# Counting the late units of a routed expert kernel in one chain of narrow steps, and turning the third unit's rows two products later

## The chip, the cores and the metric

The kernel runs on one core of a Trainium2 chip. The metric is the device time of one execution in microseconds (us). Three executions of the kernel before took 648.83, 647.14 and 644.44 us; their median is 647.14 us. A further execution was profiled. TensorE is called PE here, VectorE DVE, ScalarE ACT, GpSimd POOL and SyncE SP, as the profile does.

## The reference

An attention block feeds a mixture-of-experts block. All is float32.

```python
# attention: q, k, v are (8, 8, 576, 64); heads 0-3 see the last 32 positions,
# heads 4-7 every fourth of the last 128
attn = softmax(where(mask, q @ k.T / 8, -1e9));  x = (attn @ v) as (8, 576, 512)
# experts: 8 of them, w1 (8, 512, 1024), w2 (8, 1024, 512)
logits = x @ w_gate;  local = sigmoid(x @ w_local)
for b in range(8):
    prev_e = -1
    for s in range(576):
        fresh_e = argmax(logits[b, s])
        if s == 0 or local[b, s] < 0.5: e = fresh_e
        else:                           e = prev_e if prev_e >= 0 else fresh_e
        prev_e = e
        out[b, s] = softmax(logits[b, s])[e] * (relu(x[b, s] @ w1[e]) @ w2[e])
```

So each of 4608 tokens has one expert, and which one is known only once the attention of its batch is done, and for a later token only once its predecessors are.

## The kernel before, in words

**Stages.** First comes the attention, over eight batches. Rows of x go to DRAM (`xd`). After every two batches a group of tokens is routed (`route(g)`, four groups): logits, argmax, the carrying of an expert along a batch, and a running count of tokens for each expert. Then the experts' work is done in units. A unit is a set of rows of one expert, gathered from `xd` by an indirect DMA on POOL's queue (`fetch`, L948 to L961: a one-element memset on DVE, L959, that orders the transfer, and the transfer, L960). Its rows are turned so that features lie along partitions (`turn_rows`, L975: for units 0 to 3 eight PE transposes, L992, into a PSUM bank and one ACT copy, L993, for each 128 rows), multiplied by w1 (`hidden`), by w2 (`output`), scaled by the gate and sent to DRAM with an indirect DMA (`send`).

**Units.** A pair is 256 rows of an expert, a full 128, a half 64, a quarter 32. Pairs use a scheme with seven block products in place of eight (`chain`, L1005): each needs sums of blocks of the weights (`sums_of_weights`), of the rows (`sums_of_rows`, tile `xc`, L924 to L927) or of the hidden values (`hc`), made by DVE. Unit 1 is a pair whose hidden product is the plain one (L1072 to L1082; eight steps m0 to m7, each eight records of the trace). Units 0 and 1 ("early", `FIRST = 2`) are pairs chosen after half of the tokens are routed, so that PE has work while the routing of the last group goes on. All others are "late": 14 pairs, 3 fulls, 2 halves and 4 quarters at most.

**Counting.** `count(late)`, a generator, works out which segment of 128 rows of which expert is which unit's. On every partition stands one pair of expert and segment, and the eight counts lie along the free dimension, so nearly all its instructions have 8 elements. The late one first makes four counts for each expert (pairs, fulls, halves, quarters; L659 to L702), then decides for the partition's own segment (L714 to L738) which column of the table it is, and writes rows of zeros with one 1 (`chosen`). In it each kind has its own scan and its own chain of comparisons, on all 8 experts, and the partition's own expert is picked at the end by a product with a 0/1 row (`C_OF`) and a reduction (L734, L735). `table` then makes PE multiply `chosen` by the experts' numbers (`ep`, L748 and L750), `tokens` multiplies it by the lists of rows (`fp`, L801 to L809), and DVE turns that into row numbers (L816 to L833), which the gathers of units 2 and 3 take. `places` (`fq`, L766; L779 to L784) does so for the gathers of unit 4 and on.

**Order.** On PE and DVE the order of instructions is the order in which the program issues them; ACT, POOL and SP are ordered by the planner. The small steps of routing stand in two lists, `waiting` and `behind`, and `gap()` pops one gather (`fetch_some`) and one step of each. `work_gap` is called after each step of `hidden` and `output`; it first pops one or two sums of blocks from the list `soon`. So the late routing is spread over the steps of units 0 and 1: `total(g)` falls after the sixth product of unit 0's hidden, the first part of `count` after m1 of unit 1, the second part after m2, `table` after m5, `tokens` after m6, `places` after the first of the seven output products of unit 1. While these products run, `k` counts them from 0; at `k == 4` `feed()` (L1388) calls `features(FIRST)`: unit 2's rows are turned and their sums made.

```python
        waiting.extend(... + of(carry) + of(total)
                       ...
                       + now(counted_on) + now(sum_up, *[counted_on] * (PASSES if exact else 1)) + pause * 2
                       + now(lambda: table(True)) + now(late_tokens) + pause + now(places))
```

The whole program exists twice; the second copy (`exact`) is run only if a check on sizes and sums fails.

Of the kernel before, what the change touches and what calls it, by code (L numbers as in the profile page):

```python
# [11 lines left out]
F32 = mybir.dt.float32  # L12
# [101 lines left out]
C_AT = C_UP + 1  # L114
C_PAY = C_AT + 4
C_COL = C_PAY + NG * NJ
C_ALL = C_COL + TRIES


def constants():  # L120

    c = np.zeros((P, C_ALL), np.float32)
    c[:, C_ID:C_TRI] = np.eye(P)
    c[:TB, C_TRI:C_IDX] = np.triu(np.ones((TB, TB)), 1)
    c[:, C_IDX:C_REV] = np.arange(E)
# [87 lines left out]
def whole(ctx, tc, exact, bad, qk, v, wgl, w1, w2, con, msk, qmk, out, cst, wg, ones):  # L213
# [431 lines left out]

    tiles = {}

    def count(late):

        w = "late" if late else "early"  # L650

        def number(name, dtype=F32, shape=[P, E]):
            return sm.tile(shape, dtype, name=f"{name}_{w}")
# [4 lines left out]
        ni, nf = number("ni", I32), number("nf")  # L658
        nc.vector.tensor_scalar(ni, cn, float(ROW - 1) if late else 0.0, None, Alu.add)  # L659
        if late:  # L660
            ki, kf = number("ki", I32), number("kf")
            nc.vector.tensor_scalar(ki, cn, float(SQ - 1), None, Alu.add)
            nc.vector.tensor_scalar(ki, ki, 5, None, Alu.logical_shift_right)
            tiles["over"] = over = sm.tile([1, 5], F32, name="over_late")
            most = sm.tile([1, 1], F32, name="most")
            nc.vector.tensor_reduce(most, cn[0:1], axis=AX.X, op=Alu.max)
            nc.vector.tensor_scalar(over[:, 4:], most, float(SEGS * P), None, Alu.is_gt)
        nc.vector.tensor_scalar(ni, ni, 8, None, Alu.logical_shift_right)
        nc.vector.tensor_copy(nf, ni)
        parts = [nf]  # L670
        if late:

            nc.vector.tensor_copy(kf, ki)
            nc.vector.scalar_tensor_tensor(kf, nf, -8.0, kf, Alu.mult, Alu.add)
            full, half, quart = (number(name) for name in ("full", "half", "quart"))
            nc.vector.tensor_scalar(full, kf, 4.0, None, Alu.is_ge)
            nc.vector.scalar_tensor_tensor(kf, full, -4.0, kf, Alu.mult, Alu.add)
            nc.vector.tensor_scalar(half, kf, 2.0, None, Alu.is_ge)
            nc.vector.scalar_tensor_tensor(quart, half, -2.0, kf, Alu.mult, Alu.add)
            nc.vector.tensor_scalar(quart, quart, 0.0, None, Alu.max)  # L680
            left = number("left")
            nc.vector.tensor_tensor(left, nf, tiles["done"], op=Alu.subtract)
            parts = [left, full, half, quart]
        ends, befs = [], []
        for k, part in enumerate(parts):
            ends.append(number(f"end{k}"))
            nc.vector.tensor_tensor_scan(ends[k], part, part, 0.0, Alu.add, Alu.max)
            befs.append(number(f"bef{k}"))
            nc.vector.tensor_tensor(befs[k], ends[k], part, op=Alu.subtract)
        if late:  # L690
            for k, most in enumerate((PAIRS, FULL, HALF, QUART)):
                nc.vector.tensor_scalar(over[:, k:k + 1], ends[k][0:1, E - 1:], float(most), None, Alu.is_gt)
        if not late:
            tiles["done"] = done = number("done")
            nc.vector.tensor_scalar(done, befs[0], -1.0, float(FIRST), Alu.mult, Alu.add)
            nc.vector.tensor_scalar(done, done, 0.0, None, Alu.max)
            nc.vector.tensor_tensor(done, done, nf, op=Alu.min)
            first, ends = None, [(done, befs[0], 0)]
        else:
            first = tiles["done"]  # L700
            nc.vector.tensor_tensor(befs[0], befs[0], first, op=Alu.subtract)
            nc.vector.scalar_tensor_tensor(befs[3], half, float(E), befs[3], Alu.mult, Alu.add)  # L702
            ends = [(nf, befs[0], 0), (full, befs[1], C_FULL), (half, befs[2], C_HALF)]
        cols = TRIES if late else 2 * FIRST
        tiles["chosen", late] = []
        for turn in range(PASSES if exact and late else 1):
            yield
            seg = cst[:, C_S:C_V]
            if turn:
                seg = number("seg", F32, [P, 2])  # L710
                nc.vector.tensor_scalar(seg, cst[:, C_S:C_V], float(turn * SEGS), None, Alu.add)
            seg, seg1 = seg[:, 0:1], seg[:, 1:2]
            to, twice, is_it = number("to"), number("twice"), number("is")
            nc.vector.tensor_scalar(to, befs[0], 2.0, seg1, Alu.mult, Alu.add)  # L714
            if late:
                nc.vector.tensor_scalar(twice, first, 2.0, None, Alu.mult)
                nc.vector.scalar_tensor_tensor(to, twice, seg, to, Alu.is_le, Alu.mult)
            nc.vector.tensor_scalar(twice, ends[0][0], 2.0, None, Alu.mult)
            nc.vector.scalar_tensor_tensor(to, twice, seg, to, Alu.is_gt, Alu.mult)
            for part, bef, c in ends[1:]:  # L720
                nc.vector.scalar_tensor_tensor(is_it, twice, seg, part, Alu.is_equal, Alu.mult)
                nc.vector.scalar_tensor_tensor(is_it, bef, float(c + 1), is_it, Alu.add, Alu.mult)
                nc.vector.tensor_tensor(to, to, is_it, op=Alu.add)
                if c == C_FULL:
                    nc.vector.tensor_tensor(twice, twice, part, op=Alu.add)
            chosen = number(f"chosen{turn}", F32, [P, 2, cols])
            tiles["chosen", late].append(chosen)
            all_of = [(to, 0, C_QUART if late else cols, number("one", F32, [P, 1]))]
            if late:
                nc.vector.scalar_tensor_tensor(is_it, twice, seg, quart, Alu.is_equal, Alu.mult)  # L730
                nc.vector.scalar_tensor_tensor(is_it, befs[3], float(C_QUART + 1), is_it, Alu.add, Alu.mult)
                all_of.append((is_it, C_QUART, TRIES, number("one_quart", F32, [P, 1])))
            for to, a, z, one in all_of:
                nc.vector.tensor_tensor(to, to, cst[:, C_OF:C_S], op=Alu.mult)  # L734
                nc.vector.tensor_reduce(one, to, axis=AX.X, op=Alu.add)  # L735
                for v in range(2):
                    nc.vector.tensor_scalar(chosen[:, v, a:z], cst[:, C_COL + a:C_COL + z], one,
                                            cst[:, C_V + v:C_V + v + 1], Alu.is_equal, Alu.mult)  # L738
        yield

    def table(late):
# [467 lines left out]
    def route(g):  # L1209
# [4 lines left out]
        counts = count(g == NG - 1)  # L1214

        def now(*fs):
            return [lambda: [f() for f in fs]]
# [10 lines left out]
        if g < NG - 1:  # L1228
# [10 lines left out]
            else:  # L1239
# [5 lines left out]
                else:  # L1245
# [255 lines left out]
```

## Time and profile before

| | before |
|---|---|
| median of three executions | 647.14 us (644.44 to 648.83) |
| profiled execution | 646.66 us |
| its span, first to last instruction | 644.9 us |
| mean granted TensorE clock | 0.988 |
| PE busy | 606.5 us (94%) |
| DVE busy | 417.6 us (65%) |
| DMA, mean rate | 217 GB/s |

The times of the trace are counted from the start of the span; 1.76 us of the execution lie outside it. Rows of the timeline give the start, the duration, the engine, the line of the program, the operation, output and inputs with their shapes, and the number of instructions merged into the row; in square brackets stands the idle time of the engine before it and what released it. A float32 matmul of the program shows as two records, a transpose as one.

### The profile page before, as it was taken

What the parts mean: (1) busy time and instruction counts of PE and PEld (TensorE: products, weight loads), DVE (VectorE), ACT (ScalarE), POOL (GpSimd) and SP (SyncE); (2) the same over time, 40 slices, a digit from 0 to 9 for tenths busy, and PEclk for the clock granted to TensorE, in tenths of its full rate; (3) what the DMA queues carried; (4) which work ended last, traced back from release to release, by engine and by line L of the source; (5) the groups of instructions that cost most, each with busy time, mean ns of one, the idle gap of its engine ahead of it and who ended that gap; (6) DMA issues with size and microseconds to landing.
All of it is one profiled execution on the core that took longest, in us unless ns stands there. A gap on an engine that the chain in (4) does not pass through costs nothing.

```text
span 644.9 us, 15442 instructions
## 1 busy us (share of the span) xinstructions
PE 606.5 (94%) x6350; PEld 532.4 (83%) x6350; DVE 417.6 (65%) x976; ACT 176.6 (27%) x320; POOL 243.6 (38%) x219
## 2 busy tenths in 40 slices
PE   6888988889989999999999999999999999999995
PEld 6776776768878899999598998995979999879984
DVE  3768989989596487672747487628292974473851
ACT  2545444353111232212122222121222211213210
POOL 3322142124003655464685435345544455001011
PEclk8999999999999999999999999999999999999998
DMA  9998989398004689677363665855453767470301
GB/s 346 412 326 292 346 279 299 122 363 319 2 33 156 217 321 354 227 257 250 116 238 108 245 240 205 296 188 193 168 187 151 279 229 260 147 270 37 137 33 42
DMA packets 29744, 140.12 MB, mean 217 GB/s; under 512 B 4892, under 2 KB 15260, under 8 KB 23136
## 3 DMA queue, kind: packets, MB, share of 16 engines
q1 hardware_dynamic: 22096, 119.89, 51.0%
q0 software_dynamic: 7568, 19.15, 8.6%
q8 instruction: 52, 0.85, 0.5%
q14 instruction: 28, 0.23, 0.1%
HBM read 145.31 MB, written 19.14 MB: 255 GB/s over the span
## 4 chain that ended last, share of the span: by engine, by line
PE 71%; DVE 15%; issue 6%; DMA 4%; POOL 2%; SPq 0%; ACT 0%; POOLq 0%; DVEq 0%
PE yp L1183 28%; PE hp L1088 20%; PE pv L404 3%; PE hp L1062 3%; PE yp L1171 3%; PE sc L342 3%; DVE pr L348 2%; PE tp L423 2%; DMA vt<-in_v_dram 2%; DVE x L409 1%; POOL xg L960 1%; PE hp L1049 1%; PE yp L1136 1%; PE hp L1039 1%; DMA out_dram<-y,corner 1%
## 5 line engine op out<-in xcount | busy, mean ns | idle before, releaser
L960 POOL DMA_INDIRECT xg<-xd,at x116 | 131.7, 1136 | 142.8 <-DVE xg L959 117.8
L1098 DVE TENSOR_TENSOR h<-hp,h 128x512 f32<-128x512 f32 x45 | 30.7, 688 | 97.2 <-PE hp L1088 97.2
L1183 PE MATMUL yp<-sum,hc 128*128 128x256 f32 x384 | 88.5, 380 | 0.0
L1088 PE MATMUL hp<-xc,sum 128*128 128x128 f32 x720 | 85.6, 275 | 0.0
L1124 POOL DMA_INDIRECT out_dram<-y,tok x35 | 46.9, 1341 | 96.8 <-DVE y L1198 44.7
L1088 PEld LDWEIGHTS hp<-xc,sum 128*128 128x128 f32 x720 | 82.9, 192 | 0.1
L1183 PEld LDWEIGHTS yp<-sum,hc 128*128 128x128 f32 x384 | 72.8, 190 | 9.9
L1198 DVE SCALAR_TENSOR_TENSOR y<-yp,gate,y 128x256 f32<-128x256 f32 x48 | 23.0, 483 | 63.5 <-issue 34.5
L1183 PE MATMUL yp<-raw,h 128*128 128x256 f32 x256 | 61.2, 382 | 0.0
L351 ACT ACTIVATE pr<-pr 128x512 f32<-128x512 f32 x64 | 43.8, 685 | 60.5 <-DVE pr L348 57.9
L1088 PE MATMUL hp<-xe,raw 128*128 128x128 f32 x480 | 58.9, 276 | 0.7 <-ACT xe L993 0.7
L1088 PEld LDWEIGHTS hp<-xe,raw 128*128 128x128 f32 x480 | 56.4, 192 | 1.8 <-ACT xe L993 1.0
L348 DVE SCALAR_TENSOR_TENSOR pr<-sc,mk 128x512 f32<-128x512 f32 x64 | 45.5, 748 | 15.6 <-PE sc L342 14.1
L1183 PEld LDWEIGHTS yp<-raw,h 128*128 128x128 f32 x256 | 47.4, 190 | 9.1 <-issue 3.3
L404 PE MATMUL pv<-vt,pr 128*64 128x65 f32 x1152 | 44.0, 230 | 9.0 <-issue 4.8
L404 PEld LDWEIGHTS pv<-vt,pr 128*64 128x64 f32 x1152 | 38.7, 142 | 12.2 <-issue 6.6
L1099 ACT ACTIVATE h<-h 128x512 f32<-128x512 f32 x45 | 28.4, 632 | 64.6 <-DVE h L1098 51.1
L1092 ACT COPY h<-hp 128x512 f32<-128x512 f32 x45 | 26.4, 586 | 62.4 <-PE hp L1088 62.4
L342 PE MATMUL sc<-kq 64*64 64x96 f32 (+3 forms) x1280 | 35.4, 248 | 6.7 <-issue 2.9
L342 PEld LDWEIGHTS sc<-kq 64*64 64x64 f32 x1280 | 29.5, 138 | 12.4 <-DVE pr L348 4.4
L283 POOL COPY vt<-vt 64x1040 f32<-64x1040 f32 x16 | 16.8, 1052 | 60.6 <-DMA vt<-in_v_dram 46.6
L1191 ACT ACTIVATE y<-yp,gate 128x256 f32<-128x256 f32 x48 | 22.8, 475 | 61.0 <-PE yp L1183 61.0
(248 smaller groups left out, 956.5 us busy)
## 6 DMA issues: line engine op xcount, KB each, us to landing
raw<-in_w_dram SPq DMA_DIRECT2D x50, 2048.0 KB
kq<-in_qk_dram SPq DMA_DIRECT2D x13, 1184.0 KB
vt<-in_v_dram SPq DMA_DIRECT2D x15, 650.0 KB
xd<-x SPq DMA_DIRECT2D x16, 512.0 KB
kq<-in_qk_dram SPq DMA_DIRECT2D x6, 592.0 KB
xg<-xd,at POOLq DMA_INDIRECT x116, 4.3
xd<-x SPq DMA_DIRECT2D x32, 32.0 KB
vt<-in_v_dram SPq DMA_DIRECT2D x2, 325.0 KB
```

The source lines that it names most:

```text
L342: nc.tensor.matmul(sc[c:c + QB, u, lo - a * QB:hi - a * QB], lhsT=kt[h, WIN + j * QB:WIN + (j + 1) * QB], rhs=qt[h, lo:hi], start=True, st ...
L348: nc.vector.scalar_tensor_tensor(to, sc[:, :, :w], -CEIL, mk[:, at:at + w].unsqueeze(1).to_broadcast([P, 2, w]), Alu.max, Alu.min)
L351: nc.scalar.activation(to, to, Act.Exp, scale=SCALE)
L404: nc.tensor.matmul(pv[half * QB:(half + 1) * QB, k - a], lhsT=pr[:, u, (i - a) * QB:(i - a + 1) * QB], rhs=vt[:, slot(i), u], start=True, ...
L960: nc.gpsimd.indirect_dma_start(out=to, out_offset=None, in_=of, in_offset=bass.IndirectOffsetOnAxis(ap=place, axis=0))
L1088: nc.tensor.matmul(to[:, m], lhsT=a[:, m, kk], rhs=b[:, kk], start=first and m == 0 and kk == 0, stop=(kk == DK // 2 - 1), skip_group_chec ...
L1092: nc.scalar.copy(at((0, 1, 3)[k]), of)
L1098: nc.vector.tensor_tensor(at(k), of, at(k), op=Alu.add)
L1099: nc.scalar.activation(at(k), at(k), Act.Relu)
L1124: nc.gpsimd.indirect_dma_start(out=rows_of_out(), out_offset=bass.IndirectOffsetOnAxis(ap=of_unit(u, "tok", j), axis=0), in_=y, in_offset= ...
L1183: nc.tensor.matmul(to, lhsT=a[:, m], rhs=b[:, m], start=first and m == 0, stop=(m == FK // 2 - 1), skip_group_check=True)
L1198: nc.vector.scalar_tensor_tensor(at(k), of, of_unit(u, "gate", k // 2), at(k), Alu.mult, Alu.add)
```

## The change

`count(late)` is split into `count_early` (as before, without the late branches) and `count_late`. The late one takes the four kinds of unit from one number for each expert by shifts and masks of integers, keeps them side by side in one tile of four times eight, and makes one scan of 32 elements over all four, restarted by a new constant row (`C_NEXT`). Then the partition's own expert is picked at once, from all eight rows (four counts and what lies before them), with one product and one reduction. What follows works on one to three elements of each partition. The part that depends only on the early units is taken out of it: `known` stands in the list behind `total`. The comparison with the room for each kind is one instruction against a new constant row and stands behind the choice. In the list of steps nothing else moves. `feed()`, and with it the turning of unit 2's rows, is called at `k == 6`, behind the last output product of unit 1, in place of `k == 4`, behind the fifth. The gathers that `work_gap` pops keep their places in the sequence.

```diff
-C_ALL = C_COL + TRIES
+C_NEXT = C_COL + TRIES
+C_ROOM = C_NEXT + 4 * E
+C_ALL = C_ROOM + 4
...
-    c[:, C_COL:] = 1 + np.arange(TRIES)
+    c[:, C_COL:C_NEXT] = 1 + np.arange(TRIES)
+    c[:, C_NEXT:C_ROOM] = np.arange(4 * E) % E > 0
+    c[:, C_ROOM:] = FULL, HALF, QUART, FIRST + PAIRS
...
-    def count(late):
...
+    def choice(chosen, v, one, a, z):
+        nc.vector.tensor_scalar(chosen[:, v, a:z], cst[:, C_COL + a:C_COL + z], one,
+                                cst[:, C_V + v:C_V + v + 1], Alu.is_equal, Alu.mult)
...
+    def known():
+
+        both = number("both", (P, 2, E))
+        nc.vector.tensor_tensor_scan(both[:, 0], tiles["done"], tiles["done"], 0.0, Alu.add, Alu.max)
+        nc.vector.tensor_copy(both[:, 1], tiles["done"])
+        nc.vector.scalar_tensor_tensor(both, both, 2.0, cst[:, C_OF:C_S].unsqueeze(1).to_broadcast([P, 2, E]), Alu.mult,
+                                       Alu.mult)
+        tiles["known"] = known = number("known", (P, 2))
+        nc.vector.tensor_reduce(known, both, axis=AX.X, op=Alu.add)
+        tiles["base"] = base = number("base", (P, 3))
+        for k, c in enumerate((C_FULL, C_HALF, C_QUART)):
+            nc.vector.memset(base[:, k:k + 1], float(c + 1))
+        tiles["from", 0] = of_segments(0)
+
+    def of_segments(turn):
...
+        nc.vector.tensor_tensor(off, tiles["known"][:, 0:1], seg[:, 1:2], op=Alu.subtract)
+        nc.vector.tensor_tensor(new, tiles["known"][:, 1:2], seg[:, 0:1], op=Alu.is_le)
+        return seg[:, 0:1], off, new
+
+    def count_late():
+
+        cn = counted_tokens(True)
+        ki, whole_ = number("ki", dtype=I32), number("parts", (P, 4, E), I32)
+        nc.vector.tensor_scalar(ki, cn, float(SQ - 1), None, Alu.add)
+        nc.vector.tensor_scalar(whole_[:, 3], cn, float(ROW - 1), None, Alu.add)
+        nc.vector.tensor_scalar(ki, ki, 5, None, Alu.logical_shift_right)
+        nc.vector.tensor_scalar(whole_[:, 3], whole_[:, 3], 8, None, Alu.logical_shift_right)
+        nc.vector.scalar_tensor_tensor(ki, whole_[:, 3], -8.0, ki, Alu.mult, Alu.add)
+        most = number("most", (1, 1))
+        nc.vector.tensor_reduce(most, cn[0:1], axis=AX.X, op=Alu.max)
+        nc.vector.tensor_scalar(ki, ki, 0.0, None, Alu.max)
+        tiles["over"] = over = number("over_late", (1, 5))
+        nc.vector.tensor_scalar(over[:, 4:], most, float(SEGS * P), None, Alu.is_gt)
+        nc.vector.tensor_scalar(whole_[:, 0], ki, 2, None, Alu.logical_shift_right)
+        nc.vector.tensor_scalar(whole_[:, 1], ki, 1, 1, Alu.logical_shift_right, Alu.bitwise_and)
+        nc.vector.tensor_scalar(whole_[:, 2], ki, 1, None, Alu.bitwise_and)
+        counts, ends = number("counts", (P, 8, E)), number("ends", (P, 4, E))
+        nc.vector.tensor_copy(counts[:, :4], whole_)
+        nc.vector.tensor_tensor_scan(ends.rearrange("p k e -> p (k e)"), cst[:, C_NEXT:C_ROOM],
+                                     counts[:, :4].rearrange("p k e -> p (k e)"), 0.0, Alu.mult, Alu.add)
+        nc.vector.tensor_tensor(counts[:, 4:], ends, counts[:, :4], op=Alu.subtract)
+        nc.vector.tensor_tensor(counts, counts, cst[:, C_OF:C_S].unsqueeze(1).to_broadcast([P, 8, E]), op=Alu.mult)
+        mine = number("own_counts", (P, 8))
+        nc.vector.tensor_reduce(mine, counts, axis=AX.X, op=Alu.add)
+        for turn in range(PASSES if exact else 1):
             yield
...
+            nc.vector.tensor_scalar(far[:, 0:1], mine[:, 3:4], 2.0, seg, Alu.mult, Alu.subtract)
+            nc.vector.scalar_tensor_tensor(to, mine[:, 7:8], 2.0, off, Alu.mult, Alu.subtract)
+            nc.vector.tensor_tensor(at, mine[:, 4:7], tiles["base"], op=Alu.add)
+            nc.vector.tensor_tensor(far[:, 1:], far[:, 0:1].to_broadcast([P, 2]), mine[:, 0:1].to_broadcast([P, 2]),
+                                    op=Alu.add)
+            nc.vector.scalar_tensor_tensor(is_pair_, far[:, 0:1], 0.0, new, Alu.is_gt, Alu.mult)
+            nc.vector.scalar_tensor_tensor(at[:, 2:], mine[:, 1:2], float(E), at[:, 2:], Alu.mult, Alu.add)
+            nc.vector.scalar_tensor_tensor(far, far, 0.0, mine[:, :3], Alu.is_equal, Alu.mult)
+            nc.vector.tensor_tensor(to, to, is_pair_, op=Alu.mult)
+            nc.vector.tensor_tensor(at, at, far, op=Alu.mult)
+            nc.vector.scalar_tensor_tensor(one, at[:, 0:1], to, at[:, 1:2], Alu.add, Alu.add)
+            chosen = choosing(True, turn, TRIES)
+            for v in range(2):
+                choice(chosen, v, at[:, 2:], C_QUART, TRIES)
+                choice(chosen, v, one, 0, C_QUART)
+            if not turn:
+                nc.vector.tensor_tensor(over[:, :4], ends[0:1, :, E - 1], cst[0:1, C_ROOM:C_ALL], op=Alu.is_gt)
         yield
...
-        waiting.extend(now(turned_back, first_best) + now(owned) + now(exponentials) + of(carry) + of(total)
+        waiting.extend(now(turned_back, first_best) + now(owned) + now(exponentials) + of(carry) + now(lambda: total(g), known)
...
     for k, fits in enumerate(output(1)):
         work_gap(fits)
-        if k == 4:
+        if k == 6:
             feed()
```

More of the change, by code (lines that the diff above doesn't have):

```diff
@@ L646, in whole, with number, counted_tokens @@
     tiles = {}
-    def count(late):
-        w = "late" if late else "early"
-        def number(name, dtype=F32, shape=[P, E]):
-            return sm.tile(shape, dtype, name=f"{name}_{w}")
+    def number(name, shape=(P, E), dtype=F32):
+        return sm.tile(list(shape), dtype, name=name)
+    def counted_tokens(late):
         cn = bank([P, E], "cn")
@@ L657, in count @@
                          start=True, stop=True)
[L658 to L667, printed above, removed]
+        return cn
@@ new lines, in choosing, with count_early @@
+    def choosing(late, turn, cols):
+        chosen = number(f"chosen{turn}_{late:d}", (P, 2, cols))
+        tiles.setdefault(("chosen", late), []).append(chosen)
+        return chosen
+    def choice(chosen, v, one, a, z):
+        nc.vector.tensor_scalar(chosen[:, v, a:z], cst[:, C_COL + a:C_COL + z], one,
+                                cst[:, C_V + v:C_V + v + 1], Alu.is_equal, Alu.mult)
+    def count_early():
+        cn = counted_tokens(False)
+        ni, nf, end, bef = number("ni", dtype=I32), number("nf"), number("end"), number("bef")
+        nc.vector.tensor_copy(ni, cn)
@@ L668, in count @@
         nc.vector.tensor_scalar(ni, ni, 8, None, Alu.logical_shift_right)
         nc.vector.tensor_copy(nf, ni)
[L670 to L703, printed above, removed]
@@ L704, in count @@
-        cols = TRIES if late else 2 * FIRST
-        tiles["chosen", late] = []
-        for turn in range(PASSES if exact and late else 1):
-            yield
[L708 to L738, printed above, removed]
@@ new lines, in count_early @@
+        nc.vector.tensor_tensor_scan(end, nf, nf, 0.0, Alu.add, Alu.max)
+        nc.vector.tensor_tensor(bef, end, nf, op=Alu.subtract)
+        tiles["done"] = done = number("done")
+        nc.vector.tensor_scalar(done, bef, -1.0, float(FIRST), Alu.mult, Alu.add)
+        nc.vector.tensor_scalar(done, done, 0.0, None, Alu.max)
+        nc.vector.tensor_tensor(done, done, nf, op=Alu.min)
+        yield
+        seg, seg1 = cst[:, C_S:C_S + 1], cst[:, C_S + 1:C_V]
+        to, twice, one = number("to"), number("twice"), number("one", (P, 1))
@@ new lines, in count_early @@
+        nc.vector.tensor_scalar(to, bef, 2.0, seg1, Alu.mult, Alu.add)
+        nc.vector.tensor_scalar(twice, done, 2.0, None, Alu.mult)
+        nc.vector.scalar_tensor_tensor(to, twice, seg, to, Alu.is_gt, Alu.mult)
+        nc.vector.tensor_tensor(to, to, cst[:, C_OF:C_S], op=Alu.mult)
+        nc.vector.tensor_reduce(one, to, axis=AX.X, op=Alu.add)
+        chosen = choosing(False, 0, 2 * FIRST)
+        for v in range(2):
+            choice(chosen, v, one, 0, 2 * FIRST)
+        yield
+    def known():
[10 more added lines that the diff above has]
+        tiles["from", 0] = of_segments(0)
@@ new lines, in of_segments @@
+    def of_segments(turn):
+        seg = cst[:, C_S:C_V]
+        if turn:
+            seg = number("seg", (P, 2))
+            nc.vector.tensor_scalar(seg, cst[:, C_S:C_V], float(turn * SEGS), None, Alu.add)
+        off, new = number(f"off{turn}", (P, 1)), number(f"new{turn}", (P, 1))
+        nc.vector.tensor_tensor(off, tiles["known"][:, 0:1], seg[:, 1:2], op=Alu.subtract)
+        nc.vector.tensor_tensor(new, tiles["known"][:, 1:2], seg[:, 0:1], op=Alu.is_le)
+        return seg[:, 0:1], off, new
@@ new lines, in count_late @@
+    def count_late():
[23 more added lines that the diff above has]
+        for turn in range(PASSES if exact else 1):
+            yield
+            seg, off, new = of_segments(turn) if turn else tiles["from", 0]
+            far, is_pair_, to, at, one = (number(n_, (P, w)) for n_, w in
+                                          (("far", 3), ("is_pair", 1), ("to_pair", 1), ("at_part", 3), ("one_late", 1)))
+            nc.vector.tensor_scalar(far[:, 0:1], mine[:, 3:4], 2.0, seg, Alu.mult, Alu.subtract)
[10 more added lines that the diff above has]
+            chosen = choosing(True, turn, TRIES)
+            for v in range(2):
+                choice(chosen, v, at[:, 2:], C_QUART, TRIES)
+                choice(chosen, v, one, 0, C_QUART)
+            if not turn:
+                nc.vector.tensor_tensor(over[:, :4], ends[0:1, :, E - 1], cst[0:1, C_ROOM:C_ALL], op=Alu.is_gt)
@@ L1213, in route @@
         lane0, lane1, segment, code, what = matrices(g)
-        counts = count(g == NG - 1)
+        counts = count_late() if g == NG - 1 else count_early()
         def now(*fs):
```

## The prediction

> **What bounds the kernel now.** I read the page first, then the list of what PE waited for, then PE's timeline around the longest of those waits with the granted clock of each stretch, and then DVE's timeline there.
>
> ```profile
> span 644.9 us, 15442 instructions
> PE 606.5 (94%) x6350; PEld 532.4 (83%) x6350; DVE 417.6 (65%) x976; ACT 176.6 (27%) x320; POOL 243.6 (38%) x219
> ```
>
> PE is busy for 94% of the span. An edit to DVE's work or to an order is then worth what PE idles for it, or runs slowly because of it, and no more. The list of PE's waits (total, times, longest) has these among its rows:
>
> ```profile
> PE ep L748 <- DVE chosen_late L737: 2.9, 1, 2.9
> PE tp L992 <- DMA xg<-xd,row: 1.9, 2, 1.5
> ...
> PE hp L1088 <- DVE xg L959: 0.9, 2, 0.4
> ...
> PE hp L1088 <- DVE h L1098: 0.6, 2, 0.4
> ```
>
> The first is the wait for late counting, the second the wait of the third unit's transposes for their gathered rows: one for each half of the change. The last two are the only waits of PE behind 214 us, 1.5 us together, and none there is for weights. So what PE gains by 214 us should reach the end. PE's timeline at the two places:
>
> ```profile
> 184.17 5.35 PE L1077 MATMUL hp<-xe,raw 128*128 128x256 f32 x24
> 192.37 0.26 PE L748 MATMUL ep<-chosen_late,cst 128*1 128x58 f32 x2 [2.86 <-DVE chosen_late L737]
> ...
> 192.60 3.31 PE L1077 MATMUL hp<-xe,raw 128*128 128x256 f32 x8
> 195.71 0.56 PE L801 MATMUL fp<-chosen_late,acc 112*128 112x84 f32 x2
> ...
> 198.59 1.89 PE L1183 MATMUL yp<-raw,h 128*128 128x256 f32 x8
> ...
> 208.27 0.60 PE L992 MATMUL tp<-cst,xg 128*128 128x128 f32 x4
> ...
> 211.20 0.41 PE L992 MATMUL tp<-cst,xg 128*128 128x128 f32 x2 [1.54 <-DMA xg<-xd,row]
> 211.44 1.89 PE L1183 MATMUL yp<-raw,hc 128*128 128x256 f32 x8
> ...
> 214.90 1.95 PE L1088 MATMUL hp<-xe,raw 128*128 128x128 f32 x16
> ```
>
> m3 to m5 of unit 1 end at 184.17 + 5.35 = 189.52, and PE stands until 192.37. Then m6, eight records, takes 195.71 - 192.60 = 3.11 us, where m3 to m5 took 5.35 / 3 = 1.78 each. The reason stands in the stretches (length, busy times, then the granted clock, third from the end):
>
> ```profile
> 193.00:194.00 1.00, 1.00 (x4) 0.79 (x3) 0.86 (x3) 0.00 (x0) 0.00 (x0) 0.56 0.00 0
> 194.00:195.00 1.00, 1.00 (x4) 0.82 (x3) 0.00 (x0) 0.00 (x0) 0.00 (x0) 0.50 0.00 0
> 195.00:196.00 1.00, 1.00 (x5) 0.82 (x4) 0.00 (x0) 0.00 (x0) 0.00 (x0) 0.50 0.00 0
> 196.00:197.00 1.00, 1.00 (x21) 0.93 (x21) 0.10 (x1) 0.00 (x0) 0.00 (x0) 0.73 0.00 0
> ...
> 210.00:212.00 2.00, 0.80 (x5) 0.78 (x6) 0.00 (x0) 0.36 (x1) 1.46 (x2) 1.00 0.36 121
> ```
>
> Right behind the 2.86 us of idling the clock is halved for 193 to 196.5 us; behind the shorter idling at 210 us it is not. The loss is 0.44 + 0.50 + 0.50 + 0.27 = 1.71 us at most.
>
> **Part one: the counting.** DVE's rows, first of the old chain, then of wider instructions elsewhere:
>
> ```profile
> 182.90 0.16 DVE L659 TENSOR_SCALAR ni_late<-cn 128x8 int32<-128x8 f32 x1
> ...
> 184.16 0.17 DVE L676 TENSOR_SCALAR full_late<-kf_late 128x8 f32<-128x8 f32 x1
> 184.37 0.17 DVE L677 SCALAR_TENSOR_TENSOR kf_late<-full_late,kf_late 128x8 f32<-128x8 f32 x1
> ...
> 184.97 0.17 DVE L680 TENSOR_SCALAR quart_late<-quart_late 128x8 f32<-128x8 f32 x1
> 185.05 0.16 DVE L682 TENSOR_TENSOR left_late<-nf_late,done_early 128x8 f32<-128x8 f32 x1
> ...
> 186.79 1.21 DVE L926 TENSOR_TENSOR sum<-raw 128x1024 f32<-128x1024 f32 x1
> ...
> 188.13 0.21 DVE L714 TENSOR_SCALAR to_late<-bef_late,cst 128x8 f32<-128x8 f32 x1
> ...
> 192.03 0.49 DVE L737 TENSOR_SCALAR chosen_late<-cst,one_quart_late 128x16 f32<-128x16 f32 x2
> 192.43 1.22 DVE L927 TENSOR_TENSOR sum<-raw,sum 128x1024 f32<-128x1024 f32 x1
> ```
> ```profile
> 173.58 0.22 DVE L590 TENSOR_TENSOR pl<-kp,oh 128x72 f32<-128x72 f32 x1
> 173.84 0.28 DVE L591 TENSOR_REDUCE pf<-pl 128x9 f32<-128x72 f32 x1
> ...
> 153.92 0.96 DVE L488 TENSOR_TENSOR eq<-eq,cst 128x72 f32<-128x72 f32 x1
> ```
> ```profile
> 150.00:154.00 4.00, 4.00 (x39) 4.00 (x38) 3.83 (x12) 1.17 (x2) 3.10 (x3) 1.00 1.01 428
> ```
> ```profile
> 199.19 1.00 POOL L960 DMA_INDIRECT xg<-xd,row  x1 [20.05 <-DVE xg L959]
> ```
>
> The first part takes 186.79 - 182.90 = 3.89 us, the second 192.43 - 188.13 = 4.30; between them lie a sum of weights and the addition to `acc`, 1.34 us, which stay. An instruction that needs its predecessor's result starts 0.21 us behind it (184.16 to 184.37), one that doesn't 0.08 (184.97 to 185.05), a 72-element one with a dependence 0.26 (173.58 to 173.84), a choice 0.20 (two between 192.03 and 192.43).
>
> The new first part has 16 instructions. Its path: the second addition starts at 0.08, then shift, `ki`, its maximum and the three masks follow (4 x 0.21 + 2 x 0.08), the last mask starting at 1.08; the conversion at 1.29; scan, subtraction, product and reduction 0.26 each, to 2.33; the next instruction 0.20 later: 2.53 us. The two tests for overflow fall into its pauses. DVE reaches L926 at 182.90 + 2.53 = 185.43 and the second part at 186.77. That has ten narrow steps: seven starts up to the comparison `far` at about 0.55, `at` 0.21 later, `one` 0.21 later, 0.13 until the first choice, four choices of 0.20, and 0.1 for the end of the last: 2.0 us. `chosen` is complete at 188.8, before PE arrives at 189.52, with 0.7 us to spare. The idling goes whole (2.86 us), and with it the slow clock, for which I take 1.6 of the at most 1.71 us (m6 alone shows 3.11 - 1.78 = 1.33). What is late next is nothing on PE: the list of rows `fp` needs `acc` copied (L803) behind one sum of 1.22 us, so by about 190.3, and PE reaches `fp` only at 189.52 + 0.23 + 1.78 = 191.5. Sum of this part: **-4.5 us**.
>
> Bounds: a faster chain gives nothing, since PE sets the time from 189.52 on. A slower one costs nothing up to 0.7 us, and all is lost at 3.6 us more. The row of L488 shows that 72 elements, one operand repeated, can take 0.96 us; it came at the end of a stretch in which POOL was busy for 3.10 of 4 us, while POOL idles for 20.05 us around late counting. I take the 0.26, since L590 and L591 are as wide and have no such neighbour.
>
> [...]
>
> **`known`, moved to an earlier gap.** Nine small instructions behind `total` of the last group. The rows there:
>
> ```profile
> 160.29 0.06 DVE L524 MEMSET ends<- 1x1 f32 x1
> 160.77 0.16 DVE L525 COPY ends<-last 1x8 f32<-1x8 f32 x1 [0.41 <-PE last L522]
> ...
> 162.92 0.29 DVE L644 TENSOR_TENSOR acc<-acc,ap 112x128 f32<-112x128 f32 x1 [1.79 <-PE ap L639]
> ```
>
> Scan, product, reduction depend on each other (3 x 0.21), the copy and three constants cost 0.08 each, two subtractions at the end about 0.3: some 1.3 us. DVE idles for 0.41 and 1.79 us here, so L525 moves to about 161.6 and the addition at 162.92 stays. I cost it at nothing; without that cover it would be the 1.3 us of DVE, and nothing of PE, whose next use of that chain lies behind two output products. The early counting is the same instructions. Cost **0**.
>
> **Part two: turning two products later.** The transposes begin at 208.27 and the sixth product at 211.44: 3.17 us, of which 1.92 are idle. With the call at `k == 6`, products six and seven (214.90 - 211.44 = 3.46 us) run at once, and the transposes stand right before unit 2's first product, which needs the copied rows. The trace has this very order for unit 0:
>
> ```profile
> 144.62 1.09 PE L992 MATMUL tp<-cst,xg 128*128 128x128 f32 x8
> ...
> 146.44 2.05 PE L1088 MATMUL hp<-xe,raw 128*128 128x128 f32 x16 [0.73 <-ACT xe L993]
> ```
> ```profile
> 145.32 1.07 ACT L993 COPY xe<-tp 128x512 f32<-128x512 f32 x2
> ```
>
> 146.44 - 144.62 = 1.82 us from the first transpose to the first product, which began only when both copies had ended (146.39). So this place costs 1.82 instead of 3.17 us: **-1.35 us**. It holds if the rows are there. The last gather's rows are used at 211.20, that is 12.6 us behind the end of m7 (198.59); the new order wants them 208.27 - 198.59 + 3.46 + 0.6 = 13.7 us behind it. The gathers are released by DVE steps that follow the row numbers and m7, so they keep their distance: 1.1 us to spare. The ones for unit 3 pass the transposes and leave earlier, which only helps; unit 1's sends keep their place beside the products that they wait for. The four short sums `xc` are now made behind the copies, beside unit 2's first product, which takes 1.95 us (the row at 214.90); only the second product wants the first of them. Bounds: with rows late by 2.5 us nothing is gained; if the product needs only the first copy, 0.5 more.
>
> **Sum.** The profiled execution took 646.66 us (span 644.9), 0.48 below the median. -4.46 - 1.35 = -5.8 us: 640.9 for it, 641.3 for the median.
>
> **The rivals.**
>
> *A, forecast:* both parts carry, 641.3.
>
> *B:* whether the clock is halved behind the idling is chance, and the timed executions mostly lack it. For it: 1.9 us at 210 us left the clock whole, so 2.86 us may lie near the edge. Against: this trace has it. Gain 2.86 + 1.35 = 4.2: 642.9. [...]
>
> *C:* the turning gains nothing, because the rows arrive later beside other transfers, or the copy waits behind ACT's scaling of the seventh product. For it: only 1.1 us to spare. Gain 4.5: 642.7. With B as well, 644.3.
>
> *D:* more than the sum: the first product waits for one copy only (0.5 us), and some of the 1.5 us of later waits fall away: about 640.0.
>
> *E, slower:* the wide and repeated operands cost what L488 shows. Place: copy, scan, subtraction, product, reduction, and the three steps on `far` and `at`. Eight at 0.96 in place of about 0.24 are 5.8 us more: `chosen` at 194.5, so PE idles from 189.52 for 5 us, 2.1 more than now, with the clock halved as before; less the 1.35 us, 647.14 + 0.8 = 647.9. It turns slower from 5 us more on. Against: POOL idles there, and the rows at 173.58 and 173.84 are as wide and take 0.22 and 0.28.
>
> *F:* the change does not do what it says, or the gain is given back where the trace shows no reason: around 647, more if a new wait comes.
>
> **How the numbers follow.** A 0.50, B 0.13, C 0.15, D 0.12, E 0.05, F 0.05. The predicted time is A's, 641.3. The three executions before lie from 2.7 below to 1.7 above their median, and about 1% (6.5 us) is what a measurement of this kernel can tell from no change. The range runs from 1 us below D (639.0) to 0.9 above B and C together (645.2); E and F and the outer executions are left out. Faster by over 1% means below 640.67, only 0.6 below A: 0.4 of A, 0.85 of D and 0.15 of B and C give 0.20 + 0.10 + 0.04, and 0.01 of F: 0.35. Slower by over 1%: 0.02 of E and 0.03 of F, 0.05. The rest, 0.60, is within 1%.
>
> **What would show it.** Right: no wait of PE for `chosen`, the clock at 1.00 from 190 to 197 us, m6 and m7 at 1.78 us each; no wait of the transposes for `xg`; instead one wait of about 0.7 us of unit 2's first product for ACT's copies; the rest of the timeline earlier by 5.8 us. Wrong: a wait for `chosen` left (the instructions of the new chain are then longer than 0.26), a wait for `xg` at the new place (C), or PE waits behind 209 us that are not in the list above.

## The result, and the profile after

| | before | changed |
|---|---|---|
| median of 14 executions | 648.61 us (644.44 to 651.20) | 641.75 us (639.29 to 645.23) |
| ratio, with its 95% interval | | 0.9908 [0.9885, 0.9931] |
| profiled execution | 646.66 us | 643.55 us |
| span of it | 644.9 us | 641.5 us |

The change makes the kernel faster by 0.9%. The ratio is that of the means, 647.95 and 641.99 us: 6.0 us (4.5 to 7.5 by the interval); the medians differ by 6.9. The forecast was 641.3 us and 5.8 us. The two profiled executions differ by only 3.1 us, and the reason is not in the stage that was changed. I cut each trace at two points, the start of unit 1's hidden product and the start of unit 2's:

| us | before | changed |
|---|---|---|
| span's start to unit 1's hidden product | 176.80 | 180.00 |
| unit 1's hidden product to unit 2's | 38.10 | 31.64 |
| unit 2's hidden product to the end | 430.0 | 429.9 |

The changed stage is 6.46 us shorter, the long rest is the same, and what runs ahead of it, mostly the attention, was 3.2 us longer in this execution. That it is not the change is argued from its spread: the unchanged kernel took 179.42 us there in its second profile (below).

The changed kernel's page, and its list of PE's waits:

```profile
span 641.5 us, 15428 instructions
PE 605.7 (94%) x6350; PEld 532.3 (83%) x6350; DVE 416.0 (65%) x965; ACT 176.3 (27%) x320; POOL 245.0 (38%) x219
```
```profile
PE pv L408 <- issue: 8.3, 5, 2.3
...
PE hp L1117 <- ACT xe L1022: 1.0, 2, 0.7
...
PE hp L1117 <- DVE xg L988: 0.9, 2, 0.4
...
PE hp L1117 <- DVE h L1127: 0.4, 1, 0.4
```

In the full list the waits for `chosen` and for the gathered rows are gone. The wait for ACT's copies, which unit 0 had already (0.7 us), has a second instance, unit 2's, of 0.24. The first row belongs to the attention, where the trace gives no releaser; it was 4.8 us in the trace before, and is one part of the later start. PE's timeline over the stage:

```profile
187.37 5.35 PE L1106 MATMUL hp<-xe,raw 128*128 128x256 f32 x24
192.64 0.26 PE L777 MATMUL ep<-chosen,cst 128*1 128x58 f32 x2
...
192.87 1.99 PE L1106 MATMUL hp<-xe,raw 128*128 128x256 f32 x8
194.70 0.35 PE L830 MATMUL fp<-chosen,acc 112*128 112x84 f32 x2
...
197.23 1.89 PE L1212 MATMUL yp<-raw,h 128*128 128x256 f32 x8
...
208.64 1.89 PE L1212 MATMUL yp<-sum,h 128*128 128x256 f32 x8
210.36 1.04 PE L1021 MATMUL tp<-cst,xg 128*128 128x128 f32 x8
211.64 2.05 PE L1117 MATMUL hp<-xe,raw 128*128 128x128 f32 x16 [0.24 <-ACT xe L1022]
```

`ep` follows m5 without idling, m6 takes 194.70 - 192.87 = 1.83 us, and the eight transposes run at once behind the seventh product; unit 2's first product starts 211.64 - 210.36 = 1.28 us behind their start. DVE's chain, from the first addition to the sum behind the last choice:

```profile
186.09 0.16 DVE L725 TENSOR_SCALAR ki<-cn 128x8 int32<-128x8 f32 x1
...
188.02 0.23 DVE L743 TENSOR_TENSOR counts<-counts,cst 128x64 f32<-128x64 f32 x1
188.28 0.22 DVE L745 TENSOR_REDUCE own_counts<-counts 128x8 f32<-128x64 f32 x1
188.42 1.22 DVE L955 TENSOR_TENSOR sum<-raw 128x1024 f32<-128x1024 f32 x1
...
189.75 0.21 DVE L751 TENSOR_SCALAR far<-own_counts,cst 128x1 f32<-128x1 f32 x1
...
191.00 0.31 DVE L667 TENSOR_SCALAR chosen<-cst,one_late 128x50 f32<-128x50 f32 x1
191.22 0.29 DVE L667 TENSOR_SCALAR chosen<-cst,at_part 128x16 f32<-128x16 f32 x1
191.42 0.30 DVE L667 TENSOR_SCALAR chosen<-cst,one_late 128x50 f32<-128x50 f32 x1
...
191.70 1.21 DVE L956 TENSOR_TENSOR sum<-raw,sum 128x1024 f32<-128x1024 f32 x1
```

The first part takes 188.42 - 186.09 = 2.33 us (3.89 before), the second 191.70 - 189.75 = 1.95 us (4.30 before).

### The profile page after: what moved, and what is told of

It is laid out like the page before. It is cut to its first block, busy times and chain, and to the rows that moved or that the text cites. A ratio compares the mean times of both kernels' runs of the same rounds, so it can differ in the third digit from the quotient of the medians.

```text
span 641.5 us, 15428 instructions
## 1 busy us (share of the span) xinstructions
PE 605.7 (94%) x6350; PEld 532.3 (83%) x6350; DVE 416.0 (65%) x965; ACT 176.3 (27%) x320; POOL 245.0 (38%) x219
## 4 chain that ended last, share of the span: by engine, by line
PE 71%; DVE 12%; issue 8%; DMA 5%; POOL 2%; SPq 1%; ACT 0%; POOLq 0%; DVEq 0%
PE yp L1212 30%; PE hp L1117 19%; PE hp L1091 3%; PE pv L408 3%; PE yp L1200 3%; PE sc L346 3%; PE hp L1106 2%; DVE pr L352 2%; DMA out_dram<-y,corner 2%; DMA vt<-in_v_dram 2%; DVE x L413 2%; POOL xg L989 2%; PE tp L427 2%; PE hp L1078 1%; PE yp L1165 1%
```

## The experiments

The first eight ran beside executions of the kernel before that took 646.8 to 648.8 us. The last four ran together on a slower chip, on which it took 662.77 us; their traces differ from the first ones mainly behind unit 2's hidden product. Where no ratio is given, only the profiled execution was taken. Stretch means the time from the start of unit 1's hidden product to the start of unit 2's: 38.10 us before, 31.64 us changed.

### One half at a time

Counting alone:

```diff
-        if k == 6:
+        if k == 4:
             feed()
```

> The changed kernel with the turning of unit 2's rows put back to its old place, behind the fifth output product (k == 4). My theory: the two halves add up, and this one is worth the 2.86 us wait and some 1.6 us of halved clock, about 4.5 us or 0.7%: ratio about 0.993; PE shows no wait for chosen, the clock is 1.00 from ep to fp, and the transposes wait for xg as before, about 1.9 us. Rival (the clock is halved by chance, not by this idling): only 2.9 us, ratio about 0.9955. Rival (the time saved comes back as a longer wait for the rows, since the rows do not come earlier): the wait for xg grows to over 4 us and the ratio is above 0.997.

Ratio 0.9925 [0.9888, 0.9962]: faster, but the interval holds both the 0.993 that was expected and the rival's 0.9955. PE did not wait for `chosen`, and m6 took 1.83 us. The transposes, back at their old place, waited for the rows:

```profile
208.71 0.41 PE L1021 MATMUL tp<-cst,xg 128*128 128x128 f32 x2 [1.58 <-DMA xg<-xd,row]
208.95 2.85 PE L1212 MATMUL yp<-raw,hc 128*128 128x256 f32 x8
211.60 2.66 PE L1212 MATMUL yp<-sum,h 128*128 128x256 f32 x8
214.10 1.95 PE L1117 MATMUL hp<-xe,raw 128*128 128x128 f32 x16
```

The wait is as long as before (1.9 us with an earlier one of 0.3), so the time saved did not come back as a longer wait. But here the sixth and seventh products take 214.10 - 208.95 = 5.15 us, where before they took 3.46: the clock was halved behind this wait (0.87 granted from 209 to 210 us, 0.50 in the next three), as it had been in the first trace behind the other. Stretch 35.19 us.

Turning alone, in the kernel before:

```diff
-        if k == 4:
+        if k == 6:
             feed()
```

> The kernel before with the one edit that unit 2's rows are turned behind the seventh output product (k == 6). My theory: the wait of the transposes for xg, 1.92 us, goes, and a wait of 0.2 to 0.7 us for ACT's copy takes its place: from the start of unit 1's output to the start of unit 2's hidden product the trace is shorter by 1.4 to 2.0 us; ratio 0.997 to 0.998. The wait for chosen stays 2.8 to 2.9 us, and if the halved clock belongs to that idling, m6 takes about 3.1 us here too; if it is chance, m6 may take 1.8. Rival (the wait only moves to the new place): the transposes wait there for xg and the ratio is 1.000.

Ratio 0.9945 [0.9918, 0.9971], a gain of 3.6 us (1.9 to 5.3), more than was expected (0.997 to 0.998); stretch 34.55 us.

```profile
195.15 0.26 PE L748 MATMUL ep<-chosen_late,cst 128*1 128x58 f32 x2 [2.84 <-DVE chosen_late L737]
...
195.38 1.99 PE L1077 MATMUL hp<-xe,raw 128*128 128x256 f32 x8
197.21 0.35 PE L801 MATMUL fp<-chosen_late,acc 112*128 112x84 f32 x2
...
212.87 1.04 PE L992 MATMUL tp<-cst,xg 128*128 128x128 f32 x8
214.15 2.05 PE L1088 MATMUL hp<-xe,raw 128*128 128x128 f32 x16 [0.24 <-ACT xe L993]
```

The new place costs 214.15 - 212.87 = 1.28 us, as in the changed kernel; before, the old one cost 3.17, so the turning is worth 1.89 us; that the times show more fits a slow clock that the old wait brought in some executions (below). And PE idles for 2.84 us ahead of `ep`, as before, yet m6 takes 1.83 us: the clock was not halved (1.00 granted from 188 to 219 us). The slow clock does not always come with that wait.

### What halves the clock

Products in place of the idling, in the kernel before:

```diff
-        ep = bank([1, cols], "ep")
+        ep = bank([P, P], "ep")
+        for _ in range(12 if late and not exact else 0):
+            nc.tensor.matmul(ep, lhsT=ones, rhs=ones, start=True, stop=True)
+        ep = ep[0:1, :cols]
```

> The kernel before with twelve additional products of the ones tile with itself (128x128 by 128x128), about 0.22 us each, on PE right ahead of the ep product, into the bank that ep then overwrites. The chain on DVE is as long as before; only PE is busy for about 2.7 us of the 2.86 in which it waited. My theory: the slow clock comes from the idling, so m6 falls from 3.1 to about 1.8 us and fp shortens, while ep starts at the same distance from m5: 1.6 us faster, ratio about 0.9975. Rival (the clock is halved by chance or by something else): m6 takes 3.1 us in this trace too, or the ratio is 1.000.

```profile
191.69 2.84 PE L747 MATMUL ep<-ones 128*128 128x128 f32 x24
194.71 0.26 PE L751 MATMUL ep<-chosen_late,cst 128*1 128x58 f32 x2 [0.18 <-DVE chosen_late L737]
...
194.94 1.99 PE L1080 MATMUL hp<-xe,raw 128*128 128x256 f32 x8
196.77 0.35 PE L804 MATMUL fp<-chosen_late,acc 112*128 112x84 f32 x2
...
212.47 0.41 PE L995 MATMUL tp<-cst,xg 128*128 128x128 f32 x2 [2.12 <-DMA xg<-xd,row]
212.71 2.99 PE L1186 MATMUL yp<-raw,hc 128*128 128x256 f32 x8
```

m6 takes 1.83 us, as expected, but the ratio is 0.9999 [0.9971, 1.0028] where 0.9975 was expected: the times don't show the 1.6 us, and the interval just fails to exclude them. In this trace the clock was halved behind the later wait instead (0.68 granted from 213 to 214 us, 0.50 in the next two), which was also 0.6 us longer.

Then the changed kernel with its chain lengthened by 13, 18 and 23 additions:

```diff
+            if not exact:
+                pad = number("pad", (P, 1))
+                nc.vector.memset(pad, 0.0)
+                for _ in range(13):
+                    nc.vector.tensor_scalar(pad, pad, 1.0, None, Alu.add)
             seg, off, new = of_segments(turn) if turn else tiles["from", 0]
```

> The changed kernel with the chain of counting made longer on purpose: thirteen dependent one-element additions on DVE ahead of its second part, about 0.2 us each, 2.6 us. My theory of the margin: chosen is complete about 0.9 us before PE arrives, so PE waits for it about 1.7 us, and the stretch from unit 1's hidden product to unit 2's (31.6 us in the changed kernel) grows by that, plus about 1.7 us if the clock is halved behind it. Rival (the margin is larger, since ep needs only a part of chosen): a wait of under 1 us.

> The same with eighteen additions, 3.6 us: a wait of about 2.7 us, near the one of the kernel before. [...] Rival (a limit of length, between 1.9 and 2.86 us, as the trace of before alone suggests; the runs so far already speak against it): it is halved.

> The same with twenty-three additions, 4.6 us: a wait of about 3.7 us. [...] Rival (the halving has nothing to do with the length of a wait): m6 takes 1.8 us.

The two rows of each that matter, `ep` with its wait and m6 (its time is the distance to the next row, 1.8 us at full clock):

```profile
193.15 0.26 PE L782 MATMUL ep<-chosen,cst 128*1 128x58 f32 x2 [1.10 <-DVE chosen L667]
...
193.38 1.99 PE L1111 MATMUL hp<-xe,raw 128*128 128x256 f32 x8
```
```profile
193.74 0.26 PE L782 MATMUL ep<-chosen,cst 128*1 128x58 f32 x2 [2.02 <-DVE chosen L667]
...
193.97 2.79 PE L1111 MATMUL hp<-xe,raw 128*128 128x256 f32 x8
```
```profile
193.07 0.26 PE L782 MATMUL ep<-chosen,cst 128*1 128x58 f32 x2 [2.97 <-DVE chosen L667]
...
193.30 3.64 PE L1111 MATMUL hp<-xe,raw 128*128 128x256 f32 x8
```

One addition costs 0.19 us (the wait grows by 0.92 and 0.95 for five more). Thirteen of them, 2.4 us, leave a wait of 1.10 (1.7 was expected), so the margin is 1.3 us, not 0.9: `ep` reads only the half of `chosen` that the first two choices write, complete at 191.00 + 0.31 = 191.31 against `ep` at 192.64. The clock stayed whole behind 1.10 us (1.00 granted from 188 to 219 us) and was halved behind 2.02 and 2.97 (0.50 from 196 to 198 us, and from 194 to 196); m6, `fp` and m7 then took 5.90 and 6.01 us where the changed kernel takes 4.36, so a halving costs 1.5 to 1.65 us here. The wait of about 3.7 us that was expected of the longest chain did not come about.

The kernel before, profiled again:

> The kernel before, unchanged, for a second profile of it. Theory of chance: the wait for chosen is 2.8 to 2.9 us and the wait of the transposes 1.6 to 2.5 us again, and the clock behind each may be halved or not, independently of the first profile; the stretch from unit 1's hidden product to unit 2's is 36.4 us plus 1.7 for each halving. The time up to unit 1's hidden product differs from the first profile by some us, as it did between the other kernels, and the time from unit 2's hidden product to the end is 430.0 to 430.4 us. Rival (the halving belongs to the wait for chosen): m6 takes 3.1 us and the products behind the transposes run at full clock, as in the first profile.

```profile
194.97 0.26 PE L748 MATMUL ep<-chosen_late,cst 128*1 128x58 f32 x2 [2.84 <-DVE chosen_late L737]
...
195.20 3.12 PE L1077 MATMUL hp<-xe,raw 128*128 128x256 f32 x8
```

Stretch 37.99 us, with the clock halved behind the wait for `chosen` (0.50 granted from 196 to 199 us) and whole behind the other, as its rival had it; what speaks against that rival is turning alone. All these profiles together: waits at `ep` of 2.84 to 2.97 us were followed by the slow clock in three of four (before, before again, the longest chain; not turning alone), one of 2.02 us was, one of 1.10 was not; the waits at the old place of the transposes, 1.9 to 2.5 us, in two of four (counting alone and the added products; not in the two profiles of before). 2.84 us without and 2.02 us with it: there is no limit of length between them. At the six waits with it, it lasted 3.40 to 3.42 us, by the granted clock of each stretch of 1 us.

The granted clock changed on a grid in the first two traces. In that of before it was halved at 12.21, 29.28 and 193.12 us, the last two 5 and 53 steps of 3.413 us behind the first; in that of the changed kernel at 11.87, 35.77 and 104.03 us, the last two 7 and 27 such steps behind the first. Each of these six halvings lasted one step; a last one, at 640.27 and 639.93 us, began 184 steps behind the first in both. The table takes the stretch of 3.41 us that ended where the clock was halved, or, where it stayed whole behind a wait, the step of the grid with the least work there (for before again, the fourth step behind the halving in the table, with steps of the same length taken there as an estimate):

| trace | stretch, us | PE busy in it, us | clock behind it |
|---|---|---|---|
| 23 additions | 189.85 to 193.26 | 0.45 | halved |
| before | 189.71 to 193.12 | 0.75 | halved |
| before again | 192.49 to 195.91 | 0.93 | halved |
| added products | 209.94 to 213.36 | 1.29 | halved |
| 18 additions | 191.60 to 195.01 | 1.39 | halved |
| counting alone | 206.32 to 209.74 | 1.53 | halved |
| before again | 209.56 to 212.97 | 2.24 | whole |
| before | 210.19 to 213.60 | 2.40 | whole |

With 13 additions and in turning alone the clock stayed at 1.00 from 188 to 219 us, so where a grid lay there was not shown. With 13 additions PE is busy for at least 2.32 us of any 3.41. In turning alone the place matters: with the whole wait in one stretch only 0.57 us of work are left in it, with a border in the middle of the wait 1.99 us on either side. So if the clock goes by the work in each such stretch, a border fell into the wait there, and the limit lies between 1.53 and 1.99 us of work at these waits. It is not sharp: in the attention the clock was halved behind 1.63 us of work (25.87 to 29.28, before) and 2.00 us (100.62 to 104.03, changed), and stayed whole behind 1.62 and 1.67 us (46.01 to 49.42 and 86.97 to 90.38, changed). From this comes an estimate, with a grid of 3.41 us slid along PE's busy times in the traces of before and of turning alone, the limit at 1.53 or 1.99 us and every position equally likely: the wait for `chosen` brings a halving in 0.73 to 1.0 of the positions, the old wait of the transposes (as in the trace of before) in 0.34 to 0.73. In the changed kernel's trace no stretch of 3.41 us there has less than 3.17 us of work, and the clock stayed at 1.00 from 188 to 219 us.

### The place of the turning, and of `known`

```diff
-        if k == 6:
+        if k == 5:
             feed()
```

> The changed kernel with the turning of unit 2's rows one product earlier, behind the sixth (k == 5). My theory: the last gathered rows land about 12.5 us behind the end of m7 and this place wants them about 12.0 us behind it, so the transposes wait for xg for 0.3 to 1.0 us, but the seventh product covers ACT's copies and no wait for them is left: within 0.5 us of the changed kernel in the trace, ratio to the kernel before 0.990 to 0.992. Rival (the rows land earlier than thought): no wait at all, 0.4 us faster than the changed kernel.

Ratio 0.9889 [0.9857, 0.9921], not to be told from the changed kernel's; stretch 31.75 us. The transposes waited 0.32 us for the last rows, and the next product hid the copies:

```profile
212.46 0.41 PE L1021 MATMUL tp<-cst,xg 128*128 128x128 f32 x2 [0.32 <-DMA xg<-xd,row]
212.71 1.89 PE L1212 MATMUL yp<-sum,h 128*128 128x256 f32 x8
```

The rows were there 212.46 - 199.92 = 12.5 us behind the end of m7, as worked out from the trace of before (12.6).

`known` back in the late chain:

```diff
-        ... + of(carry) + now(lambda: total(g), known)
+        ... + of(carry) + of(total)
...
         cn = counted_tokens(True)
+        known()
```

> The changed kernel with the nine instructions of known put back into the late chain, ahead of its first instruction. My theory: they take 0.8 us there (163.46 to 164.25 in the changed kernel's trace) and chosen was ready for ep 1.3 us before PE came (192.64 against 191.31), so PE still does not wait for chosen and the stretch from unit 1's hidden product to unit 2's stays 31.6 us: moving them earlier was not needed for the gain. Rival (the margin is the 0.7 to 0.9 us that I first worked out, or the nine cost the 1.3 us that I first took): a wait of 0.1 to 0.6 us at ep.

`ep` at 192.55 followed m5 with no wait, so in this execution the move of `known` was not needed for the gain. The stretch was 31.88 us for another reason: the last rows came 211.51 - 197.13 = 14.4 us behind m7, where the waits for them in the other traces ended 12.5 to 13.2 us behind it, and the transposes waited for them even at the new place. The last of their four gathers had started no later, 9.0 us behind m7 as in the changed kernel, so what was late was the transfer.

```profile
192.55 0.26 PE L778 MATMUL ep<-chosen,cst 128*1 128x58 f32 x2
...
211.51 0.44 PE L1022 MATMUL tp<-cst,xg 128*128 128x128 f32 x2 [0.42 <-DMA xg<-xd,row]
```

### Two attempts at more

Four PSUM banks passed over ahead of the late stage:

```diff
     banks = ctx.enter_context(tc.tile_pool(name="late_banks", bufs=8, space=PSUM, reuse_waits="tile"))
+    for _ in range(0 if exact else 4):
+        bank([P, 512], "skipped")
```

> The changed kernel with four PSUM banks of the later stage passed over before its first use, so that unit 0's first product does not take the banks in which unit 0's turned rows lay. It asks why unit 0's first product waited for both of ACT's copies (1.82 us from the first transpose) and unit 2's only for the first (1.28 us). Theory: the bank of the second transposed block, still being read by the second copy, was the one wanted next; with other banks it is about 1.3 us at unit 0 too, and the wait 0.2 to 0.3 us. Rival (the rows are tracked as one tile, or the scaling of ACT makes the difference): 1.8 us again.

The theory falls. Unit 0's first product started 148.81 - 146.99 = 1.82 us behind its transposes, as always, and the stretch was 31.64 us.

```profile
146.99 1.10 PE L1021 MATMUL tp<-cst,xg 128*128 128x128 f32 x8
148.81 2.05 PE L1117 MATMUL hp<-xe,raw 128*128 128x128 f32 x16 [0.72 <-ACT xe L1022]
```

Why unit 0 waits for both copies and unit 2 for one stays open; what was excluded is that it hangs on which banks unit 0's first product takes.

The four gathers of unit 2 at once, the turning at `k == 4`, and the banks:

```diff
         for u in range(FIRST, TURNED):
             gather(u)
+        fetch_all(FIRST)
...
-        if k == 6:
+        if k == 4:
             feed()
```

> The changed kernel with three edits: the banks passed over as in the run with other banks, unit 2's four gathers issued together right behind the row numbers, and its rows turned behind the fifth output product again (k == 4). Theory: the rows then land before PE comes to them, so that place costs only the transposes, 0.87 us in place of 1.28, and unit 0's first product starts 0.5 us earlier: the stretch from unit 1's hidden product to unit 2's is about 31.2 us, in all 0.9 us faster than the changed kernel, ratio to the kernel before about 0.990, which the times can hardly tell from the changed kernel's. Rival (four gathers in a row hold up DVE or POOL, whose steps stand in the way of the list of rows): a new wait of the transposes for xg, or of a later product, and 32 us or more.

Ratio 0.9987 [0.9962, 1.0012], where about 0.990 was expected: most of the gain is lost. The stretch of the profiled execution was 40.32 us, longer than before, and at 665.45 us it was the second slowest of twelve, so it need not be typical. The transposes did not wait, but the list of rows for the later units (`fq`) did:

```profile
PE fq L795 <- issue: 4.5, 10, 0.5
```
```profile
198.95 1.89 PE L1212 MATMUL yp<-raw,h 128*128 128x256 f32 x8
200.77 0.60 PE L795 MATMUL fq<-chosen,acc 112*32 112x42 f32 x42
...
208.20 4.21 PE L1212 MATMUL yp<-sum,hc 128*128 128x256 f32 x9
```

`fq`, 80 small products, held PE for 208.20 - 200.77 = 7.4 us where the changed kernel needs 0.85 (199.05 to 199.90), from 201.6 us on in spells of one to six products with half a microsecond between them in which the trace shows nothing that PE waited for; then the clock was halved as well (0.73 granted from 206 to 207 us, 0.50 from 207 to 213). Six gathers ran on POOL at that time one behind the other. That they are the cause is argued from the order of events and was not tried alone.

The changed kernel again, on the same chip:

> The changed kernel once more, on the same chip as the last one, for the comparison and for a second profile. Theory: the stretch from unit 1's hidden product to unit 2's is 31.6 us, the clock is 1.00 throughout it, the rest to the end 429.9 to 430.4 us, and the time up to unit 1's hidden product differs by some us from the first profile's 180.0; ratio 0.989 to 0.993. Rival (the stretch varies as much as the start does): a length more than 0.3 us off.

Ratio 0.9910 [0.9888, 0.9932], the same as in the first comparison. Stretch 31.63 us, full clock throughout. The rest was 445.2 us rather than 430, with waits ahead of hidden products that the first traces had not:

```profile
PE hp L1117 <- issue: 4.8, 5, 2.1
PE hp L1117 <- ACT h L1121: 4.5, 2, 4.0
```

So the expected length of the rest holds for the faster chip only; why the other is slower there was not looked into.

## Why the prediction was right, and where it was not

**What bounds the kernel: right.** In the first two traces and in those of the first eight runs the time behind unit 2's hidden product is 429.9 to 430.4 us, so what PE gained ahead of it reached the end whole.

**The counting, -4.46 us: right for the trace of before, its second term wrong as a rule.** The path was worked out at 2.53 and 2.0 us and measured 2.33 and 1.95. The wide steps took 0.18 to 0.23 us each, nothing like the 0.96 of rival E, and the three on `far` and `at` 0.15 to 0.16. The margin, 0.7 us, measured 1.3, because `ep` needs only the first half of `chosen`. The 2.86 us went whole. The step that failed is "and with it the slow clock, for which I take 1.6 of the at most 1.71 us": the halving does not come with every such wait, since turning alone kept it, 2.84 us, and had full clock; by the estimate above it hangs on where the wait lies on the grid. By that estimate the term is 1.2 to 1.6 us on average. Rival B named the chance, but only for this wait; that the wait of the transposes runs the same risk, which the change also removes, was left out altogether, 0.6 to 1.2 us by the estimate. The two slips point in opposite directions.

**`known`: right, and cheaper.** Its nine instructions took 0.8 us, not 1.3, and DVE still idled 1.51 us ahead of the addition to `acc`. The run with `known` in the late chain shows that the cover was not even needed.

**The turning, -1.35 us: the mechanism right, its size off.** The mis-sized term is the 1.82 us taken over from unit 0: it measured 1.28, since unit 2's first product waits only for the first copy. The place gained 1.89 us, which is the "0.5 more" of the bounds and of D. Of C, the condition is real: the rows were 1.1 us ahead of need by the sum, and in one of the traces they came late: a wait of 0.42 us, which made the stretch 0.24 us longer.

**The sum.** Free of halved clocks the stretch was about 36.45 us before (38.10 - 1.63 and 37.99 - 1.55) and is 31.64: 4.8 us, which are 2.86 + 1.89 and a rest of 0.06. With the estimated 1.2 to 1.6 and 0.6 to 1.2 us of halvings that makes 6.6 to 7.6 us; the time gained is 6.0 us (4.5 to 7.5). The interval is too wide to settle how often each halving comes. That the forecast gain of 5.8 us came out so near owes something to luck: 1.6 us of certain clock loss and 0.5 too little at the turning stand in for two chances. That 641.3 lies so near to 641.75 owes more to it: the forecast started from 647.14 us, the median of three executions, and with the 648.61 of fourteen the same gain would have given 642.8.

## What to carry to other kernels

Price a wait on PE at its length plus the chance of a halved clock behind it, and don't read from one profile that it always or never comes: look where the wait lies on the grid of the clock's changes. Here, at the two waits, the clock was halved behind steps of 3.41 us with 1.88 us of idling and more, and stayed whole behind those with 1.17 and 1.01; in the attention it went either way at 1.8 us. Where two profiled executions are compared, cut them at the same instructions on both sides of the change: here the whole spans differ by 3.4 us, the changed stage by 6.5. And a step that follows a load should stand where the load has landed and something hides its copy; once both waits were below half a microsecond, moving it one product earlier changed nothing that could be measured.

## What the runs showed that I had not expected

The clock was halved behind a wait of 2.02 us and not behind one of 2.84. The time ahead of unit 1's hidden product was 176.8 to 182.7 us in the first two traces and those of the first eight runs, a spread almost as large as the whole effect of the change. And 80 small products on PE, 0.85 us long, took 7.4 us in one execution in which four gathers had been issued together ahead of them, with 4.5 us of waits that have no releaser in the trace.
